# Moving key and query transpositions behind the denominators in VectorE's hand-written order (attention and MLP on one core)

## The chip, the cores and the metric

One NeuronCore of one Trainium2 chip runs the whole program. The metric is the device time of one execution in microseconds (us). The kernel before takes 322.11 us, the median of 3 runs (322.04 to 322.13).

## What is computed

A causal attention with a forgetting gate, over 8 batches of 8 heads, sequence 576, head size 64, and then a two-layer MLP (512 to 2048 to 512, tanh-GELU) on the 4608 rows that come out:

```python
scores = scale * np.matmul(q, k.transpose(0, 1, 3, 2))
cum = np.cumsum(np.log(np.clip(f, 0.0001, 1.0)), axis=-1)
decay = cum[:, :, :, None] - cum[:, :, None, :]
scores = np.where(causal, -1000000000.0, scores + decay)
attn = np.exp(scores - max); attn = attn / (attn.sum + 1e-09)
x = matmul(attn, v)                      # to (4608, 512)
h = x @ w_in
g = 0.5 * h * (1.0 + np.tanh(c * (h + 0.044715 * h * h * h)))
out = g @ w_out
```

## The kernel before

**Tiling.** Four heads of one batch make a quad; there are 16, and quad i uses the buffers of index i % 2 of everything that is kept twice (`q_c`, `k_c`, `qT`, `kT`, `vw`, `pt`). The MLP goes over 9 chunks of 512 rows. Attention of the later quads is laid between the matrix products of the earlier chunks.

**Order by hand.** All of the kernel is recorded in a fixed order. The strings `FRONT` and `TABLES` are lists of words; `run` (L778) looks each word up in `ops` (L730) and records its instructions. The engines run at the same time, but each takes its own instructions strictly in the order in which they were recorded, and semaphores between engines hold what needs another's result. So to move a word in the string is to move its instructions in the queues of the engines that it uses, past the words on the same engines alone.

**The words that matter here.** The digit after the name is the quad.

- `LQ.i`, `LK.i` (L191): GpSimd issues the DMA of the queries or keys of quad i into `q_c` or `k_c`. `LX`, `LV` (L168) load values, from GpSimd's queue and SyncE's; a `@word` after it makes the first of them wait for the DMA of that word.
- `TQ.i`, `TK.i` (L197): one VectorE transposition of 32x32 blocks, `q_c` to `qT`, `k_c` to `kT`. It needs the load, and the scores of quad i-2 to have been read; the loads of quad i+2 into the same buffer need it.
- `S.i.r` (L261, L269): the scores of round r: small matmuls on TensorE into two PSUM tiles (pool `psS`, two buffers), and the exponentials of both on ScalarE into `pt`. `H.i.r.g` is the same for one pair of heads, with one PSUM tile.
- `M.i.r` (L275): causal masks on GpSimd, in place in `pt`. `m.i.r` (L304): the same by a product with a triangle on VectorE.
- `VW.i` on GpSimd and `vw.i` on VectorE (both L214): the values times the gates. `CL.i` (L219): VectorE copies 64 rows of that to the place for the shifted block of keys; here it is called the value copy.
- `D.i`: the denominators. TensorE sums `pt` over the keys (L329, with `w_bf`) into the tile `po`, of which its PSUM pool has one; VectorE transposes `po` (L348, `den`), takes the reciprocal (L350) and transposes it back, spread out (L352, `rb`).
- `V.i.x` and `v.i.x` (L329, with `vw`): the attention output of one half of the head size on TensorE, into the same `po`, or for `v` into a tile of the scores' pool `psS`; VectorE multiplies it by `rb` into `xT` (L360). Since there is one `po`, the first matmul of a `V` behind a `D` waits until L348 has read `po`, and the next product waits until L360 has.
- `F.0.n`, `f.0.n` (L635, L640, L641): n steps of the second MLP product of chunk 0 on TensorE (`f` takes the 128 columns in four groups of 32), the copy out of PSUM on VectorE, and the store from SyncE's queue.
- `I.1.p` (L374, L381): two of the 16 tiles of the first MLP product of chunk 1, with the GELU on ScalarE. `U` (L534), `G` (L544 to L550), `K` (L421): sums of blocks on VectorE for the products of chunk 1 that are done with seven instead of eight multiplications.

Of the kernel before, what the change touches and what calls it, by code (L numbers as in the profile page):

```python
# [16 lines left out]
def kernel(  # L17
# [10 lines left out]
    nc = tc.nc  # L28

    B, H, S, D = q.shape  # L30
    BH = B * H
    NT = (S + 127) // 128
# [8 lines left out]
    NQ = BH // 4  # L41
# [25 lines left out]
    LOW, HIGH = NT, NT - 1  # L67
# [7 lines left out]
        H.1.0.0 vw.1.0 M.1.0.1 M.1.0.0 WI.3 WI.4 WI.5 D.0.0 B.2.384 H.1.1.1 V.0.0.0 H.0.1.1 V.0.1.0 H.0.1.0 D.1.0 B.1.384 V.1.0.0 M.0.1 WI.6 WI.7  # L75
        H.1.1.0 M.1.1 V.1.1.0 Q.0.3.0 vw.0.1 h.0.0.0 h.0.0.0 M.0.3 LQ.2 LK.2 Q.1.3.1 h.0.0.1 h.0.0.1 S.1.2 M.1.3 VW.1.1 WO.0 D.0.1 j.0.1 j.0.1 j.0.1
        j.0.1 E.0.0 j.0.1 V.0.1.1 V.0.0.1 D.1.1 J.0.2 WO.1 V.1.1.1 V.1.0.1 J.0.3 J.1.0 WO.2@WI.7 WO.3 J.1.1 TQ.2 LK.3 LQ.3 J.1.2 J.1.3 LX.1.0@WO.0
        LQ.4 TK.2 X F.0.6 LK.4 TK.3 S.2.0 M.2.0 LK.5 F.0.10 S.2.2 M.2.2 LX.1.1@WO.2 F.0.9 S.2.1 TQ.3 F.0.10 LV.2.0@LK.5 m.2.1 vw.2 TQ.4 TK.4 S.3.0
        f.0.1 CL.2 LQ.5 VW.3 D.2 f.0.6 S.3.1 F.0.6 V.2.0 m.3.0 S.3.2 TK.5 LK.6 M.3.2 f.0.7 V.2.1 CL.3 S.4.1 m.3.1 LQ.6 F.0.6 TQ.5 H.4.2.1 D.3
        H.4.0.1 LQ.7 VW.4 H.4.0.0 V.3.1 v.3.0 f.0.3 H.4.2.0 CL.4 I.1.0 m.4.1 U.0 LV.2.1@LQ.5 I.1.4 TQ.6 m.4.2.3 I.1.1 I.1.5 U.1 LV.3.0@LQ.7 LV.3.1  # L80
        m.4.2.2 TK.6 G.0 M.4.0 LK.7 LQ.8 LK.8 I.1.2 I.1.3 U.3 K.1.0 K.1.1 K.1.2 I.1.6 I.1.7 G.1.1.2 U.2 X F.1.16 S.5.0 f.1.26 S.5.1 D.4 M.5.0 f.1.16
        S.5.2 V.4.0 m.5.2.3 f.1.10 VW.5 V.4.1 K.1.3 CL.5 m.5.2.2 S.6.0 f.1.10 M.5.1 D.5 f.1.7 S.6.1 V.5.1 f.1.12 V.5.0 T.2 S.6.2 vw.6
    """

    HOMES = {1: 0, 3: 1, 0: 2}
# [41 lines left out]
    def many(n, shape, dtype, name):  # L127
        return [singles.tile(shape, dtype, name=f"{name}{i}") for i in range(n)]
# [10 lines left out]
    vw = many(2, [128, NT + 1, 4, D], BF16, "vw")  # L139
# [9 lines left out]
    wT = singles.tile([128, NQ, NT, 4], FP32, name="wT")  # L149
    w_bf = singles.tile([128, NQ, NT + 1, 4], BF16, name="w_bf")  # L150
# [523 lines left out]
    def zeros(which):  # L674

        todo = [(w_bf[0:64, :, LOW, :], idle[0:64, 0:BH].rearrange("p (i h) -> p i h", h=4))]
        todo += [(t_[0:64, LOW, :, :], idle[0:64, 0:256].rearrange("p (h d) -> p h d", h=4)) for t_ in vw]
        todo += [(t_[64:128, HIGH, :, :], idle[64:128, 0:512].rearrange("p (h d) -> p h d", h=H)) for t_ in v_nat]
        for n in which:
            nc.scalar.copy(*todo[n])  # L680
# [39 lines left out]
        by_columns[:] = [True] * tiled  # L720
        pull(fills.setdefault(c, seven_products(c) if c else mlp_out(c)), n)

    def cast_w(copy):
        copy(w_bf[:, :, 0:NT, :], wT)
        copy(w_bf[64:128, :, LOW, :], wT[0:64, :, 0, :])

    def load_values(b, half):
        return load_v(b, 4 * half, 4)

    ops = {  # L730
        "W": lambda: cast_w(nc.vector.tensor_copy),
        "w": lambda: cast_w(nc.scalar.copy),
        "Z": lambda *which: zeros(which),
        "CU": within_tiles,
        "CW": make_w,
# [119 lines left out]
```

## Time and profile before

| | before |
|---|---|
| median of 3 runs | 322.11 us |
| the profiled execution, its time | 321.83 us |
| its span, first to last instruction | 320.1 us |
| granted TensorE clock | 1.00 |
| TensorE busy | 314.1 us, 98% |
| VectorE busy | 252.4 us, 79% |
| ScalarE busy | 208.5 us, 65% |
| GpSimd busy | 112.8 us, 35% |

The busy share is an average over the whole span. The change touches the stretch from about 48 to 64 us, where the attention of quads 2 and 3 and the first scores of quad 4 are laid between the steps of chunk 0. In that stretch the engines stand like this:

| us of the span | TensorE | VectorE | ScalarE | GpSimd |
|---|---|---|---|---|
| 48 to 52 | 4.00 | 4.00 | 2.07 | 2.83 |
| 52 to 56 | 3.72 | 3.87 | 2.85 | 1.24 |
| 56 to 60 | 4.00 | 3.94 | 3.03 | 3.37 |
| 60 to 64 | 3.87 | 3.83 | 2.76 | 2.64 |

Each number is the busy time of the engine in 4 us. A matmul's end is modelled in the profile, so a busy TensorE may hold short waits; the start of the next matmul tells more. Times below are counted from the start of the span.

### The profile page before, as it was taken

Reading aid. Unit: us, or ns where it says so; the run is one execution under the profiler, and the core shown is the slowest. Engines: PE = TensorE matmul, PEld = TensorE weight load, DVE = VectorE, ACT = ScalarE, POOL = GpSimd, SP = SyncE. Lnnn points to the kernel's source line nnn. Section 1 sums busy time; section 2 is a strip of 40 time slices with the busy share of each in tenths; the row PEclk is TensorE's granted clock in tenths of the full one; section 3 lists DMA queues with packets and bytes.
Section 4 is the critical chain, followed back from the end, with each engine's and each line's share of the span. In section 5 each row is a group of like instructions: output and inputs, shape, how many; then the busy total and the mean of one; then the engine's idle time right before and its main releaser. Section 6 shows DMA issues by size and latency. Waiting matters only on the chain.

```text
span 320.1 us, 12371 instructions
## 1 busy us (share of the span) xinstructions
PE 314.1 (98%) x5545; PEld 219.4 (69%) x5545; DVE 252.4 (79%) x398; ACT 208.5 (65%) x265; POOL 112.8 (35%) x160
## 2 busy tenths in 40 slices
PE   8999999999999999999999999999999999999995
PEld 3467744545776477766777677768766798788784
DVE  5876049986789899779987898689868969886882
ACT  5895686776766785759756865778567844722730
POOL 8897465730500219601770068204710240000000
PEclk9999999999999999999999999999999999999999
DMA  7999999898204830791159512971120112002013
GB/s 128 237 149 205 207 236 249 147 186 178 59 4 123 146 63 31 142 224 35 39 98 197 107 37 69 195 137 37 37 68 0 37 36 68 3 34 100 0 35 98
DMA packets 47573, 33.45 MB, mean 104 GB/s; under 512 B 29856, under 2 KB 42272, under 8 KB 47520
## 3 DMA queue, kind: packets, MB, share of 16 engines
q0 software_dynamic: 9712, 15.99, 29.0%
q1 hardware_dynamic: 37664, 16.60, 20.0%
q8 instruction: 43, 0.70, 1.0%
q14 instruction: 10, 0.08, 0.1%
q10 hardware_dynamic: 144, 0.07, 0.1%
HBM read 36.85 MB, written 9.44 MB: 145 GB/s over the span
## 4 chain that ended last, share of the span: by engine, by line
PE 92%; DVE 4%; DMA 1%; ACT 1%; issue 1%; DVEq 0%
PE ps_w L565 30%; PE ps_h L374 16%; PE po L329 9%; PE ps_s L261 9%; PE ps_cd L433 8%; PE ps_ab L433 6%; PE ps_h L491 4%; PE pso L635 2%; PE ps_h L388 2%; PE po_m L315 2%; PE idle_ps L239 1%; DMA gsum<-in_f_dram 1%; DVE pt L304 1%; DVE qT L197 1%; DVE kT L197 1%
## 5 line engine op out<-in xcount | busy, mean ns | idle before, releaser
L269 ACT ACTIVATE pt<-ps_s 128x1024 bf16<-128x1024 f32 (+2 forms) x98 | 92.3, 992 | 35.9 <-PE ps_s L261 32.4
L275 POOL TENSOR_SCALAR_AFFINE_SELECT pt<-pt 128x512 bf16<-128x512 bf16 (+2 forms) x67 | 39.8, 605 | 103.8 <-ACT pt L269 102.7
L374 PE MATMUL ps_h<-xT,w_in_sb 128*128 128x512 bf16 x240 | 55.1, 379 | 0.0
L565 PEld LDWEIGHTS <-gT 128*32 128x32 bf16 (+1 forms) x1247 | 50.6, 97 | 6.0 <-issue 1.7
L565 PE MATMUL ps_w<-w_out_sb,gT 128*32 128x256 bf16 (+1 forms) x1050 | 46.9, 273 | 0.0
L381 ACT ACTIVATE gT<-ps_h 128x1024 bf16<-128x1024 f32 x30 | 30.6, 1021 | 17.2 <-PE ps_h L374 16.7
L565 PEld LDWEIGHTS <-gsum 128*32 128x32 bf16 (+1 forms) x1256 | 39.2, 97 | 1.4
L374 PEld LDWEIGHTS <-w_in_sb 128*128 128x128 bf16 x240 | 23.4, 98 | 24.3 <-issue 0.4
L261 PE MATMUL ps_s<-qT,kT 32*128 32x448 bf16 (+5 forms) x880 | 35.7, 263 | 0.5 <-ACT pt L269 0.5
L214 POOL TENSOR_TENSOR vw<-v_nat,wT 128x1280 bf16<-128x1280 f32 (+1 forms) x13 | 29.8, 2292 | 4.4 <-DMA v_nat<-in_v_dram 3.9
L565 PE MATMUL ps_w<-usum,gsum 128*32 128x256 bf16 (+1 forms) x832 | 30.6, 273 | 0.0
L197 DVE STREAM_TRANSPOSE kT<-k_c 128x576 f32<-128x576 f32 x16 | 19.9, 1244 | 11.8 <-DMA k_c<-in_k_dram 11.8
L261 PEld LDWEIGHTS <-kT 32*128 32x128 bf16 x896 | 16.3, 93 | 17.6 <-issue 12.1
L442 ACT ACTIVATE gT<-snap 128x512 bf16<-128x512 f32 x45 | 26.1, 624 | 3.0 <-DVE snap L456 2.4
L590 DVE TENSOR_TENSOR o_st<-ps_w,snap 128x512 f32<-128x512 f32 x31 | 21.3, 686 | 8.4 <-PE ps_w L565 7.2
L433 PEld LDWEIGHTS <-w_in_sb 128*128 128x128 bf16 x240 | 23.4, 98 | 6.2 <-issue 1.5
L329 PE MATMUL po<-pt,vw 128*32 128x64 bf16 (+4 forms) x624 | 22.5, 278 | 0.4 <-DVE den L348 0.3
L329 PEld LDWEIGHTS <-vw 128*32 128x32 bf16 x672 | 14.5, 97 | 10.6 <-issue 4.4
L360 DVE TENSOR_TENSOR xT<-po,rb 128x576 bf16<-128x576 f32 x26 | 19.5, 750 | 2.9 <-PE po L329 2.2
L433 PEld LDWEIGHTS <-xT 128*128 128x128 bf16 x180 | 17.6, 98 | 5.2
L197 DVE STREAM_TRANSPOSE qT<-q_c 128x576 f32<-128x576 f32 x16 | 19.9, 1242 | 0.4 <-DMA q_c<-in_q_dram 0.4
L191 POOL DMA_DIRECT2D k_c<-in_k_dram x16 | 9.2, 578 | 25.0 <-DVE qT L197 21.0
(111 smaller groups left out, 488.3 us busy)
## 6 DMA issues: line engine op xcount, KB each, us to landing
out_dram<-o_st SPq DMA_DIRECT2D x35, 256.0 KB, 2.3
k_c<-in_k_dram POOLq DMA_DIRECT2D x16, 288.0 KB, 6.5
q_c<-in_q_dram POOLq DMA_DIRECT2D x16, 288.0 KB, 6.2
v_nat<-in_v_dram SPq DMA_DIRECT2D x16, 256.0 KB, 6.9
v_nat<-in_v_dram SPq DMA_DIRECT2D x20, 128.0 KB, 5.1
w_in_sb<-in_moe_w_in_dram POOLq DMA_DIRECT2D x8, 256.0 KB, 6.9
w_out_sb<-in_moe_w_out_dram POOLq DMA_DIRECT2D x4, 512.0 KB, 9.9
v_nat<-in_v_dram POOLq DMA_DIRECT2D x9, 128.0 KB, 6.0
```

Of the source, the lines that this page charges most:

```text
L197: nc.vector.transpose(out=dst.rearrange("p s c -> p (s c)").bitcast(FP32) .rearrange("p (t a) -> p a t", a=S // 32), in_=src.rearrange("p ...
L214: eng.tensor_mul(vw[i % 2][:, t0:t1], vb[:, t0:t1, h0:h0 + 4, :], wT[:, i, t0:t1, :].unsqueeze(3).to_broadcast([128, t1 - t0, 4, D]))
L261: nc.tensor.matmul(tiles[h // 2][:, h % 2, c0:c0 + nq], key_columns(i, key, h, c), qq[32 * h:32 * h + 32, q0:q0 + nq, c], start=(c == 0 an ...
L269: nc.scalar.activation(p[:, 2 * g:2 * g + 2, off:off + n], t[:, :, 0:n], AF.Exp, scale=scale)
L275: nc.gpsimd.affine_select(out=x, in_=x, compare_op=ALU.is_ge, fill=0.0, base=0, pattern=pattern, channel_multiplier=-1)
L329: nc.tensor.matmul(po[r0:r0 + w.shape[-1], 448 + q0:448 + q0 + nq], w, p[:, h, col:col + nq], start=(key in (0, "low")), stop=(key in ("lo ...
L374: nc.tensor.matmul(ph[:, j, :], w_in_sb[:, dt, 128 * ft:128 * ft + 128], xT[:, dt, CH * c:CH * (c + 1)], start=(dt == 0), stop=(dt == N_DT ...
L381: nc.scalar.activation(gT[:, 2 * pr:2 * pr + 2, :], ph, AF.Gelu_apprx_tanh)
L433: nc.tensor.matmul(ps[:, j], w[:, dt, 128 * j:128 * j + 128], x[:, dt], start=(first and j == 0 and dt == 0), stop=(dt == 1), skip_group_c ...
L442: nc.scalar.activation(gT[:, ft:ft + 2, HC * j:HC * (j + 1)], x, AF.Gelu_apprx_tanh)
L565: nc.tensor.matmul(ps[c0:c0 + width, n, cols[0]:cols[1]], x[:, j, 128 * n + c0:128 * n + c0 + width], w[:, j, cols[0]:cols[1]], start=(fir ...
L590: nc.vector.tensor_add(st, ps, kept[name])
```

## The change

Only the order of words in `FRONT` changes, from the words of quads 2 and 3 to the first of quad 4. In words:

- `TQ.4` and `TK.4` stood ahead of `S.3.0`, and so ahead of the value copy and the denominators of quad 2. Now `TQ.4` stands behind `D.2`, and `TK.4` behind `V.2.0`.
- `TK.5` stood behind `m.3.0`; now it stands ahead of it.
- `m.3.1`, the last mask product of quad 3, stood behind the value copy `CL.3`; now it stands ahead of it.
- `TQ.5` stood ahead of `D.3`; now it stands behind `v.3.0`. With it, `LQ.7`, which needs it, stands behind `VW.4` on GpSimd.

On VectorE the order from the value products of quad 2 to the store copy behind quad 3 is then:

```
before: vw.2 TQ.4 TK.4 CL.2 D.2 F V.2.0 m.3.0 TK.5 V.2.1 CL.3 m.3.1 TQ.5 D.3 V.3.1 v.3.0 F
after:  vw.2 CL.2 D.2 TQ.4 F V.2.0 TK.4 TK.5 m.3.0 V.2.1 m.3.1 CL.3 D.3 V.3.1 v.3.0 TQ.5 F
```

(F is the copy of an output tile out of PSUM, L640.) On GpSimd the one difference is that `VW.4` runs ahead of the issue of `LQ.7`. On TensorE, ScalarE and SyncE the instructions stand in the same order as before. `cast_w` gets an argument that no word uses, and records the same two copies as before.

```diff
-        LQ.4 TK.2 X F.0.6 LK.4 TK.3 S.2.0 M.2.0 LK.5 F.0.10 S.2.2 M.2.2 LX.1.1@WO.2 F.0.9 S.2.1 TQ.3 F.0.10 LV.2.0@LK.5 m.2.1 vw.2 TQ.4 TK.4 S.3.0
-        f.0.1 CL.2 LQ.5 VW.3 D.2 f.0.6 S.3.1 F.0.6 V.2.0 m.3.0 S.3.2 TK.5 LK.6 M.3.2 f.0.7 V.2.1 CL.3 S.4.1 m.3.1 LQ.6 F.0.6 TQ.5 H.4.2.1 D.3
-        H.4.0.1 LQ.7 VW.4 H.4.0.0 V.3.1 v.3.0 f.0.3 H.4.2.0 CL.4 I.1.0 m.4.1 U.0 LV.2.1@LQ.5 I.1.4 TQ.6 m.4.2.3 I.1.1 I.1.5 U.1 LV.3.0@LQ.7 LV.3.1
...
+        LQ.4 TK.2 X F.0.6 LK.4 TK.3 S.2.0 M.2.0 LK.5 F.0.10 S.2.2 M.2.2 LX.1.1@WO.2 F.0.9 S.2.1 TQ.3 F.0.10 LV.2.0@LK.5 m.2.1 vw.2 S.3.0 f.0.1 CL.2
+        LQ.5 VW.3 D.2 TQ.4 f.0.6 S.3.1 F.0.6 V.2.0 TK.4 S.3.2 TK.5 m.3.0 LK.6 M.3.2 f.0.7 V.2.1 m.3.1 CL.3 S.4.1 LQ.6 F.0.6 H.4.2.1 D.3 H.4.0.1 VW.4
+        H.4.0.0 V.3.1 v.3.0 TQ.5 LQ.7 f.0.3 H.4.2.0 CL.4 I.1.0 m.4.1 U.0 LV.2.1@LQ.5 I.1.4 TQ.6 m.4.2.3 I.1.1 I.1.5 U.1 LV.3.0@LQ.7 LV.3.1 m.4.2.2
...
-    def cast_w(copy):
-        copy(w_bf[:, :, 0:NT, :], wT)
-        copy(w_bf[64:128, :, LOW, :], wT[0:64, :, 0, :])
+    def cast_w(copy, rest=None):
+        i0, i1 = {None: (0, NQ), 0: (0, 2), 1: (2, NQ)}[rest]
+        copy(w_bf[:, i0:i1, 0:NT, :], wT[:, i0:i1])
+        if i1 > 2:
+            copy(w_bf[64:128, i0:i1, LOW, :], wT[0:64, i0:i1, 0, :])
```

The words from `TK.6` on are the same as before and only fall into other lines of the string.

More of the change, by code (lines that the diff above doesn't have):

```diff
@@ L77 @@
         j.0.1 E.0.0 j.0.1 V.0.1.1 V.0.0.1 D.1.1 J.0.2 WO.1 V.1.1.1 V.1.0.1 J.0.3 J.1.0 WO.2@WI.7 WO.3 J.1.1 TQ.2 LK.3 LQ.3 J.1.2 J.1.3 LX.1.0@WO.0
-        LQ.4 TK.2 X F.0.6 LK.4 TK.3 S.2.0 M.2.0 LK.5 F.0.10 S.2.2 M.2.2 LX.1.1@WO.2 F.0.9 S.2.1 TQ.3 F.0.10 LV.2.0@LK.5 m.2.1 vw.2 TQ.4 TK.4 S.3.0
-        f.0.1 CL.2 LQ.5 VW.3 D.2 f.0.6 S.3.1 F.0.6 V.2.0 m.3.0 S.3.2 TK.5 LK.6 M.3.2 f.0.7 V.2.1 CL.3 S.4.1 m.3.1 LQ.6 F.0.6 TQ.5 H.4.2.1 D.3
-        H.4.0.1 LQ.7 VW.4 H.4.0.0 V.3.1 v.3.0 f.0.3 H.4.2.0 CL.4 I.1.0 m.4.1 U.0 LV.2.1@LQ.5 I.1.4 TQ.6 m.4.2.3 I.1.1 I.1.5 U.1 LV.3.0@LQ.7 LV.3.1
-        m.4.2.2 TK.6 G.0 M.4.0 LK.7 LQ.8 LK.8 I.1.2 I.1.3 U.3 K.1.0 K.1.1 K.1.2 I.1.6 I.1.7 G.1.1.2 U.2 X F.1.16 S.5.0 f.1.26 S.5.1 D.4 M.5.0 f.1.16
-        S.5.2 V.4.0 m.5.2.3 f.1.10 VW.5 V.4.1 K.1.3 CL.5 m.5.2.2 S.6.0 f.1.10 M.5.1 D.5 f.1.7 S.6.1 V.5.1 f.1.12 V.5.0 T.2 S.6.2 vw.6
+        LQ.4 TK.2 X F.0.6 LK.4 TK.3 S.2.0 M.2.0 LK.5 F.0.10 S.2.2 M.2.2 LX.1.1@WO.2 F.0.9 S.2.1 TQ.3 F.0.10 LV.2.0@LK.5 m.2.1 vw.2 S.3.0 f.0.1 CL.2
+        LQ.5 VW.3 D.2 TQ.4 f.0.6 S.3.1 F.0.6 V.2.0 TK.4 S.3.2 TK.5 m.3.0 LK.6 M.3.2 f.0.7 V.2.1 m.3.1 CL.3 S.4.1 LQ.6 F.0.6 H.4.2.1 D.3 H.4.0.1 VW.4
+        H.4.0.0 V.3.1 v.3.0 TQ.5 LQ.7 f.0.3 H.4.2.0 CL.4 I.1.0 m.4.1 U.0 LV.2.1@LQ.5 I.1.4 TQ.6 m.4.2.3 I.1.1 I.1.5 U.1 LV.3.0@LQ.7 LV.3.1 m.4.2.2
+        TK.6 G.0 M.4.0 LK.7 LQ.8 LK.8 I.1.2 I.1.3 U.3 K.1.0 K.1.1 K.1.2 I.1.6 I.1.7 G.1.1.2 U.2 X F.1.16 S.5.0 f.1.26 S.5.1 D.4 M.5.0 f.1.16 S.5.2
+        V.4.0 m.5.2.3 f.1.10 VW.5 V.4.1 K.1.3 CL.5 m.5.2.2 S.6.0 f.1.10 M.5.1 D.5 f.1.7 S.6.1 V.5.1 f.1.12 V.5.0 T.2 S.6.2 vw.6
     """
@@ L730 @@
     ops = {
-        "W": lambda: cast_w(nc.vector.tensor_copy),
-        "w": lambda: cast_w(nc.scalar.copy),
+        "W": lambda *rest: cast_w(nc.vector.tensor_copy, *rest),
+        "w": lambda *rest: cast_w(nc.scalar.copy, *rest),
         "Z": lambda *which: zeros(which),
```

## The prediction

> **What bounds the kernel now.** First the page: busy shares, and the chain of waits by engine.
>
> ```profile
> PE 314.1 (98%) x5545; PEld 219.4 (69%) x5545; DVE 252.4 (79%) x398; ACT 208.5 (65%) x265; POOL 112.8 (35%) x160
> ...
> PE 92%; DVE 4%; DMA 1%; ACT 1%; issue 1%; DVEq 0%
> ```
>
> TensorE bounds nearly everything; VectorE sets the end for 4%, some 13 us. So I looked in the chain in order of time where VectorE's part lies (start, length, what):
>
> ```profile
> 49.98 1.25 DVE qT L197
> 51.23 1.09 DVE kT L197
> ...
> 52.59 0.80 DVE den L348
> ...
> 61.05 0.60 DVE den L348
> 61.65 0.04 issue
> 61.69 0.87 PE po L329 x24
> ```
>
> From 47.6 to 61.7 us the chain runs along VectorE alone, through the transpositions (L197) and both `den` (L348), and then returns to TensorE. It is one stretch, the one that the change reorders. That VectorE leads it does not say how much TensorE loses there; that is read from TensorE's own order (start, length, the weight loads as PEld):
>
> ```profile
> 51.68 1.47 PE L635 MATMUL pso<-w_out_sb,gT 128*128 128x512 bf16 x6
> 53.43 0.87 PE L329 MATMUL po<-pt,vw 128*32 128x512 bf16 x24 [0.28 <-DVE den L348]
> ...
> 57.67 1.47 PE L635 MATMUL pso<-w_out_sb,gT 128*128 128x512 bf16 x6
> 59.07 0.63 PE L261 MATMUL ps_s<-qT,kT 32*128 32x320 bf16 x8
> 59.62 0.92 PE L329 MATMUL po<-pt,w_bf 128*32 128x512 bf16 x24
> 60.47 1.09 PE L261 MATMUL ps_s<-qT,kT 32*128 32x64 bf16 x24
> 61.69 0.87 PE L329 MATMUL po<-pt,vw 128*32 128x512 bf16 x24
> ```
>
> ```profile
> 53.08 0.09 PEld L329 LDWEIGHTS <-vw 128*32 128x32 bf16 x1 [0.42 <-issue]
> ...
> 61.49 1.57 PEld L329 LDWEIGHTS <-vw 128*32 128x32 bf16 x48 [0.22 <-issue]
> ```
>
> Three waits of TensorE on VectorE are in it. (1) V.2.0: weights in at 53.08, first matmul at 53.43; as a check, six such matmuls at 57.67 are followed after 1.40 by the next work, and 51.68 + 1.40 = 53.08. So 0.35 us is lost. (2) D.3 takes 0.85 us to the next row (59.62 to 60.47), where V.2.0 takes 0.80 (53.43 to 54.23): 0.05 us, in the middle of it, for m.3.1, which ends at 59.88. (3) V.3.1: weights at 61.49, matmul at 61.69: 0.20 us.
>
> **The change, part by part.** It adds and removes no work: every VectorE instruction keeps its row's duration (transposition 1.24, 1.09 to the start of the next; `den` 0.78; L350 0.27; `rb` 0.78; L360 0.74; mask product 0.43; value copy 0.22 to 0.26).
>
> *Denominators of quad 2 ahead of TQ.4 and TK.4.* vw.2 ends at 50.06. CL.2 runs 50.10 to 50.32, `den` 50.35 to 51.13 (D.2's matmuls, row 49.03 + 0.85, are done by 49.9). `po` is free 1.9 us before 53.08, so wait (1) goes: 0.35 us. TQ.4 then runs 52.17 to 53.42, L640 from 53.26, L360 of V.2.0 from 54.00 (matmuls end at 53.08 + 0.87), TK.4 54.66 to 55.90. The first who needs TK.4 is S.4.1, at 57.10 - 0.35 = 56.75: cover 0.8 us. LK.6, which overwrites `k_c`, stands on GpSimd behind VW.3 until 57.05 in any case.
>
> *TK.5 ahead of m.3.0, m.3.1 ahead of CL.3.* The row behind this:
>
> ```profile
> 55.65 1.73 DVE L304 TENSOR_TENSOR pt<-pt,causal 128x512 bf16<-128x512 bf16 x1
> ...
> 54.77 2.33 POOL L214 TENSOR_TENSOR vw<-v_nat,wT 128x1280 bf16<-128x1280 f32 x1 [3.94 <-DMA v_nat<-in_v_dram]
> ...
> 57.65 1.24 POOL L275 TENSOR_SCALAR_AFFINE_SELECT pt<-pt 128x512 bf16<-128x512 bf16 x2
> ...
> 121.81 1.24 DVE L197 STREAM_TRANSPOSE qT<-q_c 128x576 f32<-128x576 f32 x1
> ```
>
> m.3.0 took 1.73 instead of 0.43: it was held until GpSimd's VW.3 ended at 57.10. TK.5 now fills that time (55.76 to 57.00), m.3.0 still ends at about 57.38, L360 of V.2.1 runs 57.30 to 58.05 (58.40 to 59.14 before). m.3.1 starts at 57.98, inside GpSimd's two masks (57.65 to 58.89): free 58.41, held by both at worst 59.3. D.3 starts at 59.62 - 0.35 = 59.27 and needs m.3.1 some 0.3 later (59.93 - 59.62), at 59.58; so wait (2) goes too, by 0.3 to 1.2 us. The value copy, at worst done by 60, is needed at 61.1.
>
> [...]
>
> *TQ.5 behind v.3.0.* D.3 starts at 59.27 and ends, 0.05 shorter, at 60.14; VectorE is idle then, `den` runs 60.19 to 60.93 and frees `po` at 60.98 (a semaphore takes 0.05: L348 at 60.89 + 0.74 against 61.69). V.3.1 no longer stands at TQ.5 but at what was hidden behind it, ScalarE:
>
> ```profile
> 57.77 3.05 ACT L269 ACTIVATE pt<-ps_s 128x1024 bf16<-128x1024 f32 x3 [0.88 <-PE ps_s L261]
> 61.20 1.94 ACT L269 ACTIVATE pt<-ps_s 128x1024 bf16<-128x1024 f32 x2 [0.38 <-PE ps_s L261]
> ```
>
> H.4.0.0 needs the PSUM tile that the third exponential (end 60.82) frees; its first matmul is at 60.87. These three exponentials follow S.4.1 and come only 0.35 earlier, so H.4.0.0 starts at 60.52 and V.3.1 0.62 behind it (61.49 - 60.87), at 61.14: 0.55 us gained, not 0.60. v.3.0 follows 0.68 later (row L329: 61.69, its `ps_o` at 62.37), at 61.82, but needs the tile of H.4.0.1. Its exponential started at 61.20 when the matmuls ended; these end 0.40 earlier, so it runs 60.80 to 61.82, and v.3.0 starts at 61.87: 62.37 - 61.87 = 0.50 us. f.0.3, H.4.2.0 and I.1.0 (64.38) follow without a wait; I.1.0 needs L360 of v.3.0, now done at 63.6.
>
> *What is late instead.* TQ.5 ends at about 64.7 (S.5.0 needs it at 80.1); LQ.7 goes out at 64.75 instead of 61.35, VW.4 runs ahead of it. M.4.0 and LK.7 behind them come some 1.1 later, LQ.8 and LK.8 up to 1.1 (issued 68.47 and 71.34 before); their data lands 6 to 7 us later and is first transposed at 106.6. SyncE's value loads behind LQ.7 (from 70.45) move by some 0.5, and its next store is at 83.5. VectorE is 0.36 late at the L640 behind v.3.0 (64.55 for 64.19), up to 1.1 if the masks of M.4.0 hold CL.4, m.4.1 and U.0. Its next sum for TensorE (L544, 72.60, behind 1.55 of idle time) waits for ScalarE, and would start at 72.1; VectorE is free at 71.05 + 1.1 = 72.15 at the latest. Nothing of that reaches TensorE, whose first matmul with such a sum is at 82.5, behind another 1.77 of idle VectorE.
>
> **The sum.** 0.35 + 0.05 + 0.20 are lost; 0.10 of the 0.60 goes to ScalarE; 0.50 remains, and behind 64.4 all follows TensorE. The profiled execution, 321.83 with a span of 320.1, would be 321.33 with a span of 319.6; the median of 322.11 lies 0.28 above the profiled one, and so I forecast 322.11 - 0.50 = 321.61 us. That is 0.16%; what a measurement of this kernel can tell from no change is about 0.2%, 0.64 us.
>
> **Rivals.**
>
> *A: ScalarE takes nothing back.* Then 0.60 and also the 0.07 by which H.4.0.0 now waits for its tile (the matmul before it starts at 60.78, and they follow by 0.03): 0.67, 321.44 us. For it: the semaphore latencies are some 0.05, as large as the margins. Against: the exponentials are 1.02 each, three in a row, and their start hangs on S.4.1, which gains 0.35 only.
>
> *B: the masks eat the rest.* If GpSimd's masks come 0.3 later and hold m.3.1 beyond 59.58, D.3 and `den` slip and only (1) remains: 0.35, 321.76 us. For it: L304 has been held for 1.3 us before. Against: the margin of 0.3 is already at the worst.
>
> *C: slower, the keys of quad 4 come late.* TK.4 leaves 51.07 for 54.66, inside VW.3. If VW.3 holds it as it held m.3.0, it ends at 57.10 + 1.24 = 58.34, S.4.1 starts at 58.39 instead of 57.10, and 1.29 is lost: 323.40 us. It decides from an end of TK.4 behind 56.7. Against it: the transposition at 121.81 took 1.24 wholly inside a GpSimd multiplication (120.86 to 123.19). [...]
>
> *D: nothing happens*, since VectorE owes the same work: 322.1 us. Against: VectorE idles 2.37 us before 47.64 and 1.55 before 72.60, so the debt has room.
>
> **How the numbers follow.** Forecast 0.64 (321.61), A 0.20 (321.44), B 0.07, C 0.06, D 0.03. A lies at the border: two thirds of it are faster by over 0.2%, and a tenth of the forecast: 0.13 + 0.07 = 0.20 faster. C is slower, with 0.01 of D: 0.07. The rest, 0.73, is within 0.2%. The range goes from a little beyond A, 321.37, to beyond B, 321.95; C and D are left out.
>
> **What would show it.** In the profile after: the first matmul of V.2.0 within 0.05 behind its weights at 53.08; D.3 at about 59.27; H.4.0.0 right behind an exponential's end; I.1.0 at 63.88 instead of 64.38; the L544 at about 72.1, still waiting for ScalarE. Wrong would be a transposition of quad 4 longer than 1.25 us, S.4.1 waiting for VectorE, or an I.1.0 that came 0.5 earlier with an end that did not.

## The result, and the profile after

The changed kernel takes 325.34 us (median of 20 runs, 321.16 to 327.56), the kernel before, run beside it, 322.28 us (20 runs, 320.71 to 327.58). The ratio is 1.0057, with a 95% interval of 1.0036 to 1.0078: slower, where 0.16% faster was forecast. The ratio leaves out runs that lie over 1.5% above the fastest of their kernel; the one such run that was profiled, below, shows the same cause, so the medians of all runs, 0.9% apart, are given too.

The profiled execution took 323.61 us with a span of 321.9, and is a mild one. First VectorE in the changed stretch (start, length, engine, line, operation, out<-in). The copy of the kernel before comes first, then the kernel after:

```profile
59.17 0.26 DVE L219 COPY vw<-vw 64x256 bf16<-64x256 bf16 x1
```

```profile
51.35 0.78 DVE L348 STREAM_TRANSPOSE den<-po 128x576 f32<-128x576 f32 x1
...
55.67 2.33 DVE L197 STREAM_TRANSPOSE kT<-k_c 128x576 f32<-128x576 f32 x2
57.84 1.51 DVE L304 TENSOR_TENSOR pt<-pt,causal 128x512 bf16<-128x512 bf16 x1
59.28 0.74 DVE L360 TENSOR_TENSOR xT<-po,rb 128x576 bf16<-128x576 f32 x1
59.94 0.41 DVE L304 TENSOR_TENSOR pt<-pt,causal 128x512 bf16<-128x512 bf16 x1
60.38 2.24 DVE L219 COPY vw<-vw 64x256 bf16<-64x256 bf16 x1
62.66 0.78 DVE L348 STREAM_TRANSPOSE den<-po 128x576 f32<-128x576 f32 x1
```

The order is that of the change, and the transpositions keep their 1.2. But the value copy CL.3 (L219) takes 2.24 us, where it took 0.26 before. It also starts late: m.3.0 (57.84), which the prediction had ahead of the two masks, is held by them and ends 0.28 us behind them, and that pushes m.3.1 and the copy back. Beside them, GpSimd, before and then after:

```profile
61.35 0.53 POOL L191 DMA_DIRECT2D q_c<-in_q_dram  x1 [1.97 <-DVE qT L197]
61.90 2.35 POOL L214 TENSOR_TENSOR vw<-v_nat,wT 128x1280 bf16<-128x1280 f32 x1
```

```profile
57.83 1.24 POOL L275 TENSOR_SCALAR_AFFINE_SELECT pt<-pt 128x512 bf16<-128x512 bf16 x2
59.01 0.55 POOL L191 DMA_DIRECT2D q_c<-in_q_dram  x1
60.09 2.45 POOL L214 TENSOR_TENSOR vw<-v_nat,wT 128x1280 bf16<-128x1280 f32 x1 [0.53 <-DMA v_nat<-in_v_dram]
67.54 0.59 POOL L191 DMA_DIRECT2D q_c<-in_q_dram  x1 [5.00 <-DVE qT L197]
```

VW.4 (L214) now begins at 60.09 instead of 61.90, since LQ.7 with its wait for TQ.5 no longer stands ahead of it. It ends at 62.54, and the copy ends 0.08 behind it. TensorE pays:

```profile
54.08 0.87 PE L329 MATMUL po<-pt,vw 128*32 128x512 bf16 x24
...
60.27 0.86 PE L329 MATMUL po<-pt,w_bf 128*32 128x512 bf16 x24
61.06 1.14 PE L261 MATMUL ps_s<-qT,kT 32*128 32x64 bf16 x24
63.49 0.87 PE L329 MATMUL po<-pt,vw 128*32 128x512 bf16 x24 [1.29 <-DVE den L348]
```

V.2.0 (54.08) has no wait left, and D.3 takes 0.79 (60.27 to 61.06): the first two waits of the prediction are gone. The third, V.3.1 for `den`, was to go too, and has grown from 0.20 to 1.36 us (its weights are loaded at 62.13, it starts at 63.49).

How much of the 1.8 us between the two profiled spans is the change? TensorE's own order is unchanged. Its S.3.0 stands ahead of all the work that the change touches and I.1.0 behind it, so the time between their starts measures the stretch alone:

```profile
48.18 0.70 PE L261 MATMUL ps_s<-qT,kT 32*128 32x64 bf16 x24
64.38 14.04 PE L374 MATMUL ps_h<-xT,w_in_sb 128*128 128x512 bf16 x64
```

```profile
49.17 0.70 PE L261 MATMUL ps_s<-qT,kT 32*128 32x64 bf16 x24
66.18 14.04 PE L374 MATMUL ps_h<-xT,w_in_sb 128*128 128x512 bf16 x62
```

It is 16.20 us before and 17.01 after: 0.81 us more. The other 1.0 us lies ahead of S.3.0, in words that the change does not touch: in the execution after, TensorE waits 1.24 us at 22.3 behind VectorE, which had waited 1.70 us for values to land. Behind I.1.0 the two executions agree: 255.7 us to the end in both.

### The profile page after: what moved, and what is told of

The parts are those of the page before. It is cut to its first block, busy times and chain, and to the rows that moved or that the text cites. A ratio compares the mean times of both kernels' runs of the same rounds, so it can differ in the third digit from the quotient of the medians.

```text
span 321.9 us, 12349 instructions
## 1 busy us (share of the span) xinstructions
PE 312.0 (97%) x5525; PEld 219.2 (68%) x5545; DVE 253.9 (79%) x398; ACT 208.8 (65%) x265; POOL 114.0 (35%) x160
## 4 chain that ended last, share of the span: by engine, by line
PE 90%; DVE 4%; DMA 2%; ACT 1%; issue 1%; POOL 1%; DVEq 0%
PE ps_w L565 30%; PE ps_h L374 16%; PE po L329 9%; PE ps_cd L433 8%; PE ps_s L261 7%; PE ps_ab L433 6%; PE ps_h L491 4%; PE pso L635 3%; DMA v_nat<-in_v_dram 2%; PE ps_h L388 2%; PE idle_ps L239 1%; PE po_m L315 1%; DVE kT L197 1%; DVE vw L219 1%; DVE pt L304 1%
## 5 line engine op out<-in xcount | busy, mean ns | idle before, releaser
L275 POOL TENSOR_SCALAR_AFFINE_SELECT pt<-pt 128x512 bf16<-128x512 bf16 (+2 forms) x67 | 41.2, 626 | 101.6 <-ACT pt L269 100.6
L214 POOL TENSOR_TENSOR vw<-v_nat,wT 128x1280 bf16<-128x1280 f32 (+1 forms) x13 | 29.6, 2276 | 4.1 <-DMA v_nat<-in_v_dram 3.7
L360 DVE TENSOR_TENSOR xT<-po,rb 128x576 bf16<-128x576 f32 x26 | 19.6, 752 | 3.1 <-PE po L329 2.4
L433 PE MATMUL ps_cd<-xT 128*128 128x256 bf16 x120 | 18.0, 273 | 0.0
```

Source lines behind the costliest of these rows:

```text
L214: eng.tensor_mul(vw[i % 2][:, t0:t1], vb[:, t0:t1, h0:h0 + 4, :], wT[:, i, t0:t1, :].unsqueeze(3).to_broadcast([128, t1 - t0, 4, D]))
L275: nc.gpsimd.affine_select(out=x, in_=x, compare_op=ALU.is_ge, fill=0.0, base=0, pattern=pattern, channel_multiplier=-1)
L433: nc.tensor.matmul(ps[:, j], w[:, dt, 128 * j:128 * j + 128], x[:, dt], start=(first and j == 0 and dt == 0), stop=(dt == 1), skip_group_c ...
```

## The experiments

Each was run beside the kernel before. In all fifteen profiles of the study, before and after included, I.1.0 to the end took 255.7 to 255.8 us. So the stretch from S.3.0 to I.1.0 is given for each, from its one profiled execution, beside medians of the runs. "Clock" counts the runs whose mean granted TensorE clock was below 0.998. That mean is over the whole execution: in the profiles of "swap alone" and "before, filled" windows of 1 us show it at 0.50 between 11 and 16 us, far ahead of the stretch, and at 1.00 in the stretch; that of "VW.4 late, again" has a mean of 0.995 beside an undisturbed stretch of 15.70 us. So low counts say little; the high ones are to be set against the 13 of 83 of the kernel before. The rows with 321.78, 321.65, 321.69 and 321.68 in the column "before" come from four chips.

| kernel | stretch, us | median, us | before, us | ratio, 95% interval | clock |
|---|---|---|---|---|---|
| before | 16.20 | | | | 13 of 83 |
| changed | 17.01 | 325.34 | 322.28 | 1.0057 (1.0036 to 1.0078) | 13 of 20 |
| changed, again | 21.12 | 326.17 | 321.78 | none | 5 of 6 |
| VW.4 late | 15.70 | 321.59 | 321.78 | 0.9992 (0.9968 to 1.0017) | 3 of 12 |
| TQ.5 back | 15.77 | 321.51 | 321.78 | 0.9998 (0.9976 to 1.0020) | 1 of 12 |
| VW.4 early | 19.87 | 325.52 | 321.78 | 1.0140 (1.0095 to 1.0186) | 6 of 6 |
| D.2 first alone | 15.70 | 322.19 | 321.65 | 1.0009 (0.9982 to 1.0037) | 4 of 12 |
| TQ.5 behind alone | 20.25 | 325.52 | 321.65 | 1.0115 (1.0079 to 1.0150) | 5 of 6 |
| VW.4 early, filled | 18.86 | 324.74 | 321.65 | 1.0088 (1.0051 to 1.0124) | 1 of 7 |
| VW.4 in two | 19.81 | 324.99 | 321.65 | 1.0113 (1.0070 to 1.0155) | 6 of 6 |
| before, filled | 18.32 | 324.15 | 321.69 | 1.0083 (1.0051 to 1.0115) | 2 of 4 |
| copy first | 19.65 | 325.08 | 321.69 | 1.0076 (1.0042 to 1.0109) | 7 of 10 |
| swap alone | 17.04 | 322.35 | 321.69 | 1.0022 (1.0003 to 1.0041) | 3 of 10 |
| VW.4 late, again | 15.70 | 321.26 | 321.69 | 0.9984 (0.9965 to 1.0003) | 2 of 12 |
| held work taken away | 16.20 | 321.32 | 321.68 | 0.9997 (0.9974 to 1.0020) | 1 of 10 |

### The changed kernel again

> The changed kernel once more, beside the others on one chip. Theory H (the value copy CL.3 is held by VW.4): in the profile CL.3 (L219) takes about 2 us and ends just behind a GpSimd multiplication (L214) that began ahead of it, and TensorE waits 1.2 to 1.4 us for den at V.3.1; time 1 to 2 us above before. Theory F (the time is lost in the loads of the first 45 us, by chance, and the change itself gains 0.5): the quad 3 scores S.3.0 start at about the same time as in the run of before or up to 1 us off in either direction, CL.3 takes 0.25, and the median of several runs is 0.5 below before.

Its six runs: 320.90 once, and 325.83 to 326.30 five times, too few together for a ratio. So the loss is there in most executions and absent in some, with the same program. The median is 4.4 us above before, where 1 to 2 were expected. This profile is of a bad one. VectorE's m.3.1, GpSimd's two masks and VW.4, and TensorE:

```profile
57.65 4.06 DVE L304 TENSOR_TENSOR pt<-pt,causal 128x512 bf16<-128x512 bf16 x1
...
57.32 1.24 POOL L275 TENSOR_SCALAR_AFFINE_SELECT pt<-pt 128x512 bf16<-128x512 bf16 x2
58.50 0.55 POOL L191 DMA_DIRECT2D q_c<-in_q_dram  x1
59.07 2.34 POOL L214 TENSOR_TENSOR vw<-v_nat,wT 128x1280 bf16<-128x1280 f32 x1
...
58.69 0.43 PE L329 MATMUL po<-pt,w_bf 128*32 128x512 bf16 x8
61.76 1.02 PE L329 MATMUL po<-pt,w_bf 128*1 128x448 bf16 x16 [2.63 <-DVE pt L304]
62.71 1.56 PE L261 MATMUL ps_s<-qT,kT 32*128 32x64 bf16 x24
```

Here it is not the copy but m.3.1, the mask product, that is caught: first by the masks, then by VW.4, 4.06 us for 0.41 of work. D.3 stops in its middle for 2.63 us. And then TensorE is slow: H.4.0.1 and H.4.0.0 take 1.56 instead of 1.14. Which instruction is caught hangs on where VectorE stands when VW.4 begins, and that moves from one execution to the next: S.3.0 started at 47.15 to 49.67 in these profiles, and VW.4 itself came later in two of them: in the first one of the changed kernel it still waited 0.53 us for its values to land, and in "copy first" GpSimd was idle for 0.39 us ahead of it.

The clock, in stretches of 4 us (window; length; busy time and count of TensorE, its weight loads, VectorE, ScalarE, GpSimd; then the granted clock, the DMA share and GB/s):

```profile
58.00:62.00 4.00, 1.36 (x21) 0.59 (x24) 3.92 (x2) 1.80 (x2) 3.39 (x3) 0.89 0.93 144
62.00:66.00 4.00, 4.00 (x72) 1.90 (x68) 2.05 (x4) 1.94 (x2) 0.00 (x0) 0.50 0.02 3
66.00:70.00 4.00, 4.00 (x50) 1.73 (x43) 3.36 (x6) 1.15 (x2) 0.65 (x2) 0.75 0.02 4
```

TensorE is idle for 2.6 us, and the granted clock falls to 0.50. In windows of 2 us it reads 1.00, then 0.79 (60 to 62), 0.50 three times, and 1.00 again, so it is taken for 1.00 or 0.50 at any time, and the mean over each window gives the time at 0.50: (0.11 + 0.50 + 0.25) x 4 / 0.5 = 6.9 us, in which at most half, 3.4 us, of full-speed work is lost. That is an estimate of the upper end, since the clock fell at about 61.2, while TensorE was still waiting. The stretch gives what it came to: 21.12 - 15.70 (the same order without the hold, below) - 2.63 (the wait) = 2.8 us, about as much as the wait.

### Which part of the change it is

Only VW.4 is put back behind LQ.7:

```diff
-... D.3 H.4.0.1 VW.4 H.4.0.0 V.3.1 v.3.0 TQ.5 LQ.7 f.0.3 ...
+... D.3 H.4.0.1 H.4.0.0 V.3.1 v.3.0 TQ.5 LQ.7 VW.4 f.0.3 ...
```

> The changed kernel with one word moved: VW.4 back behind LQ.7 on GpSimd, so that it can't run before TQ.5 is done (about 65 us). VectorE's order is that of the change. Theory H: nothing of GpSimd stands beside CL.3, so CL.3 takes 0.2 to 0.7, V.3.1 starts without a wait for den, and the time is that of the forecast, 0.4 to 0.6 below before. Theory F: VW.4 makes no difference, the time is that of the changed kernel within 0.3. Theory L (what costs is that TQ.5, LQ.7 and all loads behind them come 3 to 6 us late): the time stays 1 us or more above before, since they stay late.

The loss is gone, with VectorE's order that of the change to the last instruction:

```profile
57.98 1.20 DVE L304 TENSOR_TENSOR pt<-pt,causal 128x512 bf16<-128x512 bf16 x1
59.21 0.22 DVE L219 COPY vw<-vw 64x256 bf16<-64x256 bf16 x1
60.33 0.78 DVE L348 STREAM_TRANSPOSE den<-po 128x576 f32<-128x576 f32 x1 [0.89 <-PE po L329]
...
65.76 2.34 POOL L214 TENSOR_TENSOR vw<-v_nat,wT 128x1280 bf16<-128x1280 f32 x1
```

m.3.1 is held for 0.8 us by the masks, as the prediction had it, the copy is not held, `den` waits for TensorE again, and VW.4 runs at 65.76. The stretch is 15.70 us: the forecast 0.50 less than before. The late LQ.7 and the loads behind it are the same as in the changed kernel, so they cost nothing.

TQ.5 and LQ.7 put back ahead, which holds VW.4 back too:

```diff
-... H.4.2.1 D.3 H.4.0.1 VW.4 H.4.0.0 V.3.1 v.3.0 TQ.5 LQ.7 f.0.3 ...
+... H.4.2.1 TQ.5 D.3 H.4.0.1 LQ.7 VW.4 H.4.0.0 V.3.1 v.3.0 f.0.3 ...
```

> The changed kernel with TQ.5 back ahead of D.3, and LQ.7 ahead of VW.4; the denominators of quad 2 first and the mask product ahead of the copy are kept. Theory H: VW.4 waits for LQ.7, which waits for TQ.5, which stands behind CL.3 on VectorE, so CL.3 can't be held; TQ.5 fills VectorE's idle time ahead of D.3's den; 0.3 to 0.6 below before. Theory L: the loads are early again, so also below before. Theory F: as the changed kernel.

The stretch is 15.77 us: TQ.5 fits ahead of `den`. Then the other way round, on the kernel before with all of VectorE's order left alone:

```diff
-... D.3 H.4.0.1 LQ.7 VW.4 H.4.0.0 ...
+... D.3 H.4.0.1 VW.4 LQ.7 H.4.0.0 ...
```

> The kernel before with one word moved: VW.4 ahead of LQ.7. VectorE's order is that of before. Theory H: VW.4 then runs from about 60 to 62.4, beside the last mask product m.3.1 or the copy CL.3 in some runs (they start at 59.2 to 60.5, with the shift of the run's first 45 us), and holds one of them to its end: up to 2 us above before where it hits, nothing where it starts behind them. Theory F and L: no difference, 0 within 0.2, since TQ.5 and the loads keep their places.

```profile
58.64 2.67 DVE L219 COPY vw<-vw 64x256 bf16<-64x256 bf16 x1
58.88 2.34 POOL L214 TENSOR_TENSOR vw<-v_nat,wT 128x1280 bf16<-128x1280 f32 x1
```

One word on GpSimd makes the kernel before 1.4% slower, 3.7 us where at most 2 were expected, and in all six runs the clock was low. Here CL.3 stands first and took 2.67 us. The part of the change that brings VW.4 forward, alone, and the first part alone:

```diff
-... F.0.6 TQ.5 H.4.2.1 D.3 H.4.0.1 LQ.7 VW.4 H.4.0.0 V.3.1 v.3.0 f.0.3 ...
+... F.0.6 H.4.2.1 D.3 H.4.0.1 VW.4 H.4.0.0 V.3.1 v.3.0 TQ.5 LQ.7 f.0.3 ...
```

> The kernel before with the last part of the change alone: TQ.5 behind v.3.0 and LQ.7 behind VW.4. Theory H: VW.4 comes early, as in the run with VW.4 alone ahead, and holds CL.3 or m.3.1 of VectorE in most runs: S.3.0 to I.1.0 18 to 20 us, the time 2 to 4 above before. If instead the early VW.4 did harm only together with the early TQ.5, it is 16.0 us, and 0.2 below before.

The stretch is 20.25 us, much as with VW.4 alone.

```diff
-... m.2.1 vw.2 TQ.4 TK.4 S.3.0 f.0.1 CL.2 LQ.5 VW.3 D.2 f.0.6 S.3.1 F.0.6 V.2.0 m.3.0 ...
+... m.2.1 vw.2 S.3.0 f.0.1 CL.2 LQ.5 VW.3 D.2 TQ.4 f.0.6 S.3.1 F.0.6 V.2.0 TK.4 m.3.0 ...
```

> The kernel before with the first part of the change alone: TQ.4 behind D.2, TK.4 behind V.2.0; all else, GpSimd's order too, as before. Theory H: V.2.0 starts without its wait of 0.35 for den, TQ.4 and TK.4 come in time for S.4.1; from the start of S.3.0 to that of I.1.0 it takes 15.8 to 15.9 us instead of 16.20; the time 0.3 to 0.4 below before. The rival that the transpositions come late for quad 4: 16.5 or more.

The first part alone gives the whole 0.50 in its profile, more than the 0.35 that the prediction gave it: with VectorE that much earlier, TQ.5 ahead of `den` delays nothing. The runs don't show it: 322.19 us against 321.65, with an interval on both sides of 1. An execution's first 48 us scatter by more than the gain (S.3.0 starts at 47.15 to 49.67), so the median over 12 runs settles neither sign.

The exchange of m.3.1 and CL.3, undone in the changed kernel and made alone in the kernel before:

```diff
-... V.2.1 m.3.1 CL.3 S.4.1 ...       (changed kernel)
+... V.2.1 CL.3 m.3.1 S.4.1 ...
...
-... V.2.1 CL.3 S.4.1 m.3.1 ...       (kernel before)
+... V.2.1 S.4.1 m.3.1 CL.3 ...
```

> The changed kernel with CL.3 ahead of m.3.1 again; VW.4 stays ahead of LQ.7. Theory H: the order of these two plays no part, whichever stands beside VW.4 is held; S.3.0 to I.1.0 17 to 21 us and 2 to 4 above before in most runs. If the swap is what costs, 15.7 us and 0.5 below before.

> The kernel before with m.3.1 ahead of CL.3 and nothing else changed. Theory H: VW.4 waits for TQ.5, both are done before it; S.3.0 to I.1.0 16.0 to 16.2 us (the 0.05 of D.3's wait may go), the time within 0.2 of before. If the swap costs by itself: 17 us or more.

Undone, the loss stays (CL.3 then takes 2.30 us beside VW.4). Made alone, it missed the expectation: 17.04 us, and a ratio of 1.0022 just clear of 1. In that execution VW.3 came late, at 57.08, since its values landed late; the masks behind it ran from 59.96 to 61.20, and they held the copy for 1.57 us. Whether the old order would have been caught as well in such an execution was not tried, so a small price of the exchange stays open.

### What holds, and what is held

> The changed kernel with VW.4 as two GpSimd instructions (two of the five key blocks, then three). If a held VectorE instruction gets in as soon as the one GpSimd instruction beside it ends, CL.3 or m.3.1 is held for at most 1.0 to 1.5 instead of up to 2.3, and the median is 1 to 3 us below that of the changed kernel. If it is held until GpSimd has nothing more to do, the split changes nothing: 325 to 326.

VW.4 as two instructions (`VW.4.0 VW.4.1` for `VW.4`) did not shorten the hold:

```profile
57.01 4.19 DVE L304 TENSOR_TENSOR pt<-pt,causal 128x512 bf16<-128x512 bf16 x1
...
56.68 1.24 POOL L275 TENSOR_SCALAR_AFFINE_SELECT pt<-pt 128x512 bf16<-128x512 bf16 x2
57.86 0.55 POOL L191 DMA_DIRECT2D q_c<-in_q_dram  x1
58.43 2.48 POOL L214 TENSOR_TENSOR vw<-v_nat,wT 128x512 bf16<-128x512 f32 x2
```

m.3.1 got in neither between the two halves, nor in the half microsecond in which GpSimd only issues a DMA (57.92 to 58.43); it ended 0.29 behind the last of them. The median, 324.99 us, is within the spread of the changed kernel.

The last run leaves VW.4 early and takes the two instructions off VectorE:

```diff
-... V.2.1 m.3.1 CL.3 S.4.1 LQ.6 ...
+... V.2.1 M.3.1 cl.3 S.4.1 LQ.6 ...
```

> The changed kernel with VW.4 as early as in it, but m.3.1 and CL.3 taken from VectorE: GpSimd does both itself (a mask as the others, a copy of 64 rows), ahead of VW.4. VectorE then has nothing but transpositions, reciprocals and products with one SBUF input beside VW.4. If only those two forms of VectorE instruction are held by VW.4 (theory H): no VectorE instruction takes longer than elsewhere, den 0.78, V.3.1 waits at most 0.6 for the masks, which come later, S.3.0 to I.1.0 15.7 to 16.6 us, granted clock at full speed in most runs, time 0.5 below to 0.4 above before. If an early VW.4 costs by itself (its reads, the loads behind it, or any VectorE instruction beside it held): 17 us or more, 2 to 4 above before.

```profile
60.71 2.33 POOL L214 TENSOR_TENSOR vw<-v_nat,wT 128x1280 bf16<-128x1280 f32 x1
...
60.41 0.78 DVE L348 STREAM_TRANSPOSE den<-po 128x576 f32<-128x576 f32 x1 [2.13 <-PE po L329]
61.22 0.27 DVE L350 RECIPROCAL rec<-den 128x18 f32<-128x18 f32 x1
61.52 0.78 DVE L352 STREAM_TRANSPOSE rb<-rec 128x576 f32<-128x576 f32 x1
62.40 0.76 DVE L360 TENSOR_TENSOR xT<-po,rb 128x576 bf16<-128x576 f32 x1
```

Four VectorE instructions lie beside VW.4 and keep their durations; 321.32 us, no loss. So an early VW.4 does no harm where the mask product and the copy are not beside it. (The two on GpSimd put VW.4 some 1.0 us later: from the first mask to the issue of LQ.6 it is 2.22 us, where it was 1.18 before. And D.3 waits for the mask and takes 1.29 us (58.99 to 60.28) instead of 0.80; that is why the stretch is 16.20 and not 15.70.)

### What the clock takes

> VW.4 ahead of LQ.7 on the kernel before, with ten more matmuls of 512 columns (0.216 us each, 2.16 in all, of zeros, into a PSUM tile that nobody reads) on TensorE ahead of D.3. Theory H with the clock: of the 3.7 us lost, some 2.5 are the wait for the held VectorE instruction and some 1.2 the half clock that follows TensorE's idle time; the extra matmuls fill the wait, the granted clock stays at 1.00, S.3.0 to I.1.0 takes 18.7 to 19.1 and the time is 0.7 to 1.5 below that of VW.4 ahead alone, though it does more. If the clock has no part in it, the added work fits into the wait and the time is the same, 325.5 within 0.4.

> The kernel before with the ten added matmuls ahead of D.3 alone, VW.4 where it was. It prices the filling: TensorE has no long wait there, so S.3.0 to I.1.0 should take 16.20 + 2.16 less what the two short waits of 0.05 and 0.20 give back, 18.1 to 18.4 us, and the time 1.9 to 2.2 above before. If TensorE waited for something that the profile doesn't show, less.

Ten matmuls `nc.tensor.matmul(ps, idle[:, 0:128], idle, start=True, stop=True)` are recorded ahead of `D.3`. On the kernel before they cost 2.12 us of the stretch. With VW.4 early they make it 1.01 us shorter, 18.86 for 19.87, and the median 0.78 lower (0.65 if each is set against the before beside it), though CL.3 is held for 2.66 us there as well. The clock was low in 1 of 7 runs instead of 6 of 6. With the filling, and without:

```profile
62.00:64.00 2.00, 1.73 (x35) 0.72 (x35) 1.97 (x3) 0.00 (x0) 0.59 (x1) 1.00 0.74 118
```

```profile
60.00:62.00 2.00, 0.18 (x4) 0.10 (x7) 1.97 (x3) 0.10 (x1) 1.22 (x1) 0.91 0.80 121
62.00:64.00 2.00, 2.00 (x38) 0.97 (x32) 1.95 (x3) 0.04 (x1) 0.59 (x1) 0.50 0.17 32
64.00:66.00 2.00, 2.00 (x52) 0.99 (x52) 1.22 (x2) 1.89 (x2) 0.03 (x1) 0.73 0.67 97
```

Without it (0.09 + 0.50 + 0.27) x 2 / 0.5 = 3.4 us run at half clock: at most 1.7 us lost. The stretch has 19.87 - 16.20 - 2.50 (the wait) = 1.2 us beside the wait, and the filling won 1.0 of it back.

### The change without the early VW.4

> The changed kernel with VW.4 behind LQ.7 once more, for a closer comparison with before. Theory H: S.3.0 to I.1.0 15.7 us against 16.20, granted clock 0.99 or less in no run, the time 0.3 to 0.6 below before. If the gain is lost behind I.1.0: from I.1.0 to the end more than the 255.7 us of all runs so far.

15.70 us again, and 321.26 us against 321.69. It beats the changed kernel clearly. Against the kernel before, two comparisons of 12 runs give 0.9992 and 0.9984, both intervals reaching 1: the gain of 0.5 us is seen in the profiles, and is not proven by the times. The expectation that no run has a clock of 0.99 or less held; two had 0.995.

## Why the prediction was wrong

**Right: the waits and their sizes.** V.2.0's wait of 0.35 and D.3's of 0.05 went in the profile after. With VW.4 out of the way the stretch is 0.50 us shorter, to the hundredth of the sum, with V.3.1 behind ScalarE and I.1.0 behind it as worked out. How the 0.50 was shared out was less right: the first part alone gave all of it, so the other parts were not needed for it. TK.4 came in time and no transposition was held (rival C); LQ.7, LQ.8 and the value loads were late and nobody waited for them; behind I.1.0 nothing changed.

**The step that failed** is "The value copy, at worst done by 60, is needed at 61.1", together with "VW.4 runs ahead of it" in the list of what is late. The second told that VW.4 moves forward on GpSimd, and gave it no price. The first looked for what could hold the copy and found only the masks, which ended at 58.89. By the rows of before the margin between the copy and VW.4 was small or none: m.3.1 and the copy done between 58.7 and 60, VW.4 free to start from 59.4, when LQ.6 is issued. In three profiles with an early VW.4 (changed, changed again, VW.4 early) it began at 60.09, 59.07 and 58.88, beside one of the two each time. The one that was caught took some 2 to 3.7 us more than its work; the longest of these was held by the masks first. That TQ.5 had kept VW.4 away, by way of LQ.7 in GpSimd's queue, was a protection that the order before contained and the change took away.

The rows of before had a hold in them: m.3.0, with two SBUF inputs, took 1.73 us for 0.43 and ended 0.28 us behind VW.3. The prediction put it to m.3.0 and to the masks, and not to the one GpSimd instruction that the change itself moves. The runs show the mask product held beside VW.4 too (up to 4.19 us for 0.41, the masks included). They show the copy, with one input, held as well (2.24 to 2.67 for 0.22). The transpositions, the reciprocal and the product L360 beside VW.4 in "held work taken away" kept their 0.78, 0.27 and 0.76 us. What in an instruction decides whether it is held is not shown.

The prediction has a transposition that was not held (rival C), and took the copy at 0.22 to 0.26. The trace before has copies that took longer. CL.4, beside two GpSimd masks, took twice its time and ended 0.08 us behind them; another copy, at 109.88, took 0.58:

```profile
64.91 0.51 DVE L219 COPY vw<-vw 64x256 bf16<-64x256 bf16 x1
...
64.19 1.15 POOL L275 TENSOR_SCALAR_AFFINE_SELECT pt<-pt 64x256 bf16<-64x256 bf16 x2
```

**A second error: one execution was taken for all.** The margins were read from a single trace, in which S.3.0 starts at 48.18. Over the profiles it starts anywhere from 47.15 to 49.67, while VW.3 (3.94 us of waiting for it before), and at times VW.4 (0.53 us after), follows the landing of a load. A margin of some tenths between two engines that no semaphore ties is no cover then. It fits that the same program gives 320.9 and 326.3; no execution near 320.9 of the changed kernel was profiled.

**A cost that no part of the sum had** is the clock. In the five profiles with a wait of 2.4 to 2.7 us, the stretch less the undisturbed one (15.70 or 16.20) and less the wait leaves 1.2 to 2.8 us for it. With the longer wait it makes the difference between the 0.81 us of the mild profile and the 3 us between the medians. Rival B had the place right (the masks, m.3.1, D.3) and the holder and the size wrong.

## What to carry to other kernels

A word moved in one queue also frees what stood behind it there: follow the instruction that now starts earlier, and ask what of the other engines it lies beside. Where GpSimd and VectorE work side by side as here, keep mask products and copies that a critical chain needs (0.41 and 0.22 us of work, up to 4.19 and 2.67 when held) away from long GpSimd instructions by an order or a wait, not by a margin that one trace shows. And price a TensorE wait as long as those here (2.4 us and more) with the granted clock of 0.50 that came with it (1.2 to 2.8 us beside the wait).

## What the runs showed of the hardware

A held VectorE instruction does not always get a turn between GpSimd instructions that follow directly. In two profiles m.3.1 got none through two masks, a DMA issue of 0.55 us and VW.4, whole or in halves: 4.06 and 4.19 us in all. But m.3.0, held by VW.3, got out during the DMA issue behind it with the masks following at once: out at 57.38 before, the masks from 57.65, and likewise in the second profile of the changed kernel (57.06, masks from 57.32) and with VW.4 early (56.85, masks from 57.12). In the profile after it got out during an issue that a wait for a load followed (59.35). What decides that is open. The end of each hold lies close behind GpSimd's last instruction: 0.08 to 0.09 us for the copy, 0.28 to 0.30 for the mask product. In the one profile with VW.4 in two, nothing got in between the halves.

The granted clock fell to 0.50 with waits of TensorE of 2.4 to 2.6 us, in the windows of three profiles: for 3.4 us with "VW.4 early" and "copy first" (waits of 2.50 and 2.36), 6.9 with "changed, again" (2.63), starting between 0.6 us before the end of the wait and 1.2 behind it. In two more, "TQ.5 behind alone" and "VW.4 in two" (2.68 and 2.44), a value product of quad 3 took 1.53 and 1.57 us instead of 0.87, as in "changed, again" at 0.50 (1.53), and the mean clock of the execution was 0.993 and 0.994. Behind the wait of 1.36 it did not fall. The length of one wait does not decide it alone: 2.50 and 2.63 us went with 3.4 and 6.9 us at 0.50, and in two profiles, "swap alone" and "before, filled", it fell at 11 to 12 us, far ahead of the stretch. With matmuls on zeros in the wait it stayed at 1.00 in the one profile taken, and in 6 of 7 runs the mean was not below 0.998.
